# Attention and gated MLP on one core: where the gain's multiplications stand in block 2, and how the last tokens of batch 0 are laid out

## The chip, the cores and the metric

The kernel runs on one core of one Trainium2 chip. A core has a matrix engine (TensorE, "PE" in the profile; its weight loads are "PEld"), three engines for elementwise work (VectorE "DVE", ScalarE "ACT", GpSimd "POOL"), a queue engine (SyncE, "SP") and 16 DMA engines that move data between device memory and the on-chip memory of 128 partitions. The products of TensorE go to PSUM, a memory of eight banks.

The metric is the device time of one execution in microseconds. The kernel before takes 338.99 us, the median of 3 runs (338.89 to 339.11).

## What is computed

```python
# q, k, v: (8 batches, 8 heads, 576 tokens, 64)   fp32;  g_norm: (64,)
kv  = einsum('bhsd,bhse->bhde', k, v)             # linear attention, no softmax
out = einsum('bhsd,bhde->bhse', q, kv)
rms = sqrt(mean(out * out, axis=-1, keepdims=True) + 1e-06)
x   = (out / rms * g_norm)                        # -> (4608 tokens, 512)
g   = x @ w_gate;  val = x @ w_val                # 512 -> 1536
ffn = (gelu(g) * val) @ w_out                     # 1536 -> 512
y   = x + sigmoid(x @ w_res) * ffn
```

The kernel works in nine blocks: block b (0 to 7) takes the first 512 tokens of batch b, and block 8 takes the last 64 tokens of all batches. `kv` needs all 576 tokens of a batch, so each batch's last 64 tokens of k and v are loaded apart. While TensorE does the MLP of one block, the other engines and some slots of TensorE do the attention of the next.

## The kernel before

The opening (batch 0). Loads are issued on the SyncE queue in this order; `th_all` is a buffer that the MLP uses later, borrowed here for the fp32 last tokens.

```python
first_raw, first_last = [], []
for which in "kv":
    t = hid_of[which]
    first_last.append(t[:, 2 * H * NJ * D :][:, 0 : 2 * H * D].rearrange("p (j h d) -> p j h d", j=2, h=H))
    first_raw.append([th_all[:, 2 * len(first_raw) + i, :] for i in range(2)])

def load_first_last(half):                      # four heads of k, and of v
    hs = slice(half * HH, (half + 1) * HH)
    for i, t in enumerate((k, v)):
        nc.sync.dma_start(                      # 32 partitions x 4 heads x (2 tokens x 64)
            out=first_raw[i][half][0 : R // 2, :].rearrange("p (h x) -> p h x", h=HH),
            in_=t[0, hs, M0:S, :].rearrange("h (p j) d -> p h (j d)", j=2),
        )

for which, t in (("q", q), ("k", k), ("v", v)):
    load_first(which, t, 0, HH)                 # heads 0 to 3, 512 KB each
    if which == "k":
        load_first_last(0)
for pr in range(NP // 2, NP):                   # head pairs 2 and 3, 256 KB each
    load_first("q", q, 2 * pr, 2 * pr + 2)
    load_first("k", k, 2 * pr, 2 * pr + 2)
    if pr == NP // 2:
        load_first_last(1)
    load_first("v", v, 2 * pr, 2 * pr + 2)
# [cut: fp32 loads of the first columns of w_gate and w_val, on the same queue]
```

The rows of `first_last` that no token fills are zeroed; a cast brings the tokens to fp16; `f_kv` sums the product over the tokens of a head pair, and `f_kv_out` keeps the two diagonal 64x64 blocks of the 128x128 result with a mask:

```python
for t in first_last:
    nc.vector.memset(t, 0.0)
# [cut]
def f_cast_last(i, half, copy):
    hs = slice(half * HH, (half + 1) * HH)
    copy(out=first_last[i].rearrange("p j h d -> p h j d")[0 : R // 2, hs, :, :],
         in_=first_raw[i][half][0 : R // 2, :].rearrange("p (h j d) -> p h j d", h=HH, j=2))

def f_kv(pr):
    # [cut: four matmuls over the first 512 tokens]
    for j in range(2):
        kl, vl = (t[:, j].rearrange("p h d -> p (h d)")[:, cs] for t in first_last)
        nc.tensor.matmul(ps, lhsT=kl, rhs=vl, start=False, stop=(j == 1))

def f_kv_out(pr):
    nc.vector.tensor_tensor(out=s0["kv2"][:, pr, :], in0=first["kv", pr], in1=mask, op=ALU.mult)
```

The order of the opening is a list of words: a name, a number (head pair, half or count) and the engine (A ScalarE, D VectorE, P GpSimd). qc, kc, vc are casts; lk, lv the casts of the last tokens; qT, qo the transpose of q and its copy; kv, kvo the product and its masked copy; o the product with q; sq, rd, rt, ri, t the normalisation; xT, xo the transpose of x; g, v the first MLP products; wg, wv, wcg, wcv loads and casts of weights; warm matmuls on zeros that keep TensorE busy.

```python
opening = """
qc1P qc0A qT1 qT0 kc1P kc0A qo0D warm3 lv0D lk0P qo1A warm3 vc1D vc0A kv1 qc2A kv0 kvo1 kvo0 o1 kc2P qT2
lk1P lv1D sq1 qo2D o0 warm3 warm2 vc2P sq0 rd1 kv2 qc3P rt1 kvo2 rd0 kc3A qT3 wg1 wv1 ri1 o2 rt0 t1 warm3 warm1 sq2 vc3D
rd2 qo3A xT1 kv3 wg2 wcg0P rt2 kvo3 ri0 ri2 warm2 o3 t2 xo1A wcg1P sq3a wcv0P sq3b g1 xT2 rd3a wcv1P rd3b
wv2 t0 xo2A wg3 wv3 v1 xT0 rt3 ri3 xo0A g2 v2 t3a t3b xT3a xT3b g0 xo3aA xo3bD gelu v0 g3a v3a g3b v3b
"""
```

A block of the MLP has 12 slots, one for each group of 128 columns. In each, TensorE makes two products (`gps`, `vps`, eight matmuls), ScalarE the gelu, VectorE the product of the two; four PSUM banks take turns. Further work is put in after a slot's own:

```python
def m_act(blk, f, gps, vps):
    nc.scalar.activation(out=ge, in_=gps, func=AF.Gelu)                        # L345
    nc.vector.tensor_tensor(out=hids[blk][:, f, :], in0=ge, in1=vps, op=ALU.mult)  # L346

def a_norm(b, j0, j1):                       # slot 7 of block 2, for batch 3
    nc.vector.tensor_scalar(out=m, in0=ss, ...)                # L275
    nc.vector.tensor_scalar(out=yy.bitcast(I32), in0=m.bitcast(I32), ...)      # L276
    # [cut: L279, then nine small instructions L281 to L283]

def a_x(b, j):                               # one row of x, times g, in place   # L317
    nc.vector.tensor_tensor(out=t_t[blk][:, jj, :], in0=t_t[blk][:, jj, :], in1=g16, op=ALU.mult)
```

Block 1's x for TensorE takes g in a transpose copy, so its rows in `t_t[1]` are without g and are multiplied only for the residual addition. Block 1's output is finished during block 2, on GpSimd (`fin`, L492), and stored:

```python
if later:                                     # block 1 alone
    at(blk + 1, 5, lambda: fin((0, 0)))       # res_all += t_t[1], rows 0 and 1
    at(blk + 1, 6, lambda: fin((0, 1)), lambda: store(0))
    at(blk + 1, 9, lambda: fin((1, 0)))       # rows 2 and 3
    at(blk + 1, 10, lambda: fin((1, 1)), lambda: store(1))
# [cut]
if blk == 2:
    for j, g in enumerate(rows):              # rows: a_x(1, 0) to a_x(1, 3)
        plan.setdefault(3 + j, []).append(g)
```

In block 2 the other additions to slots are: the kv product of batch 3 and its copy (slot 1), GpSimd's issue of batch 4's loads (slot 2), the products with q and their squares and sums (slots 2 to 5), `a_norm` (7), a sum of halves of `hid` (8, L425), and the scaling and the multiplication by g of batch 3's rows (9 and 10).

Of the kernel before, what the change touches and what calls it, by code (L numbers as in the profile page):

```python
# [8 lines left out]
FP32 = mybir.dt.float32  # L9
# [3 lines left out]
ALU = mybir.AluOpType  # L13
# [5 lines left out]
def kernel(  # L19
# [15 lines left out]
    nc = tc.nc  # L35
    P = nc.NUM_PARTITIONS
    B, H, S, D = q.shape
# [4 lines left out]
    NJ = 4  # L42
    M0 = NJ * P
    R = S - M0
    RP = R // NJ
    HH = H // 2
    WCS = (256, 256, 512, 512)

    consts = ctx.enter_context(tc.tile_pool(name="consts", bufs=1))
# [92 lines left out]
    th_all = finp.tile([P, NJ, C], FP32, bufs=1, name="th")  # L142
# [634 lines left out]
    for which in "kv":  # L777
        if which == "k":
            t = hidp.tile([P, NF, NJ * P], FP16, tag="hid", name=which + "f").rearrange("p a b -> p (a b)")
        else:  # L780
            t = hid_s
# [7 lines left out]
    first_raw, first_last = [], []  # L789
    for which in "kv":  # L790
        t = hid_of[which]
        first_last.append(t[:, 2 * H * NJ * D :][:, 0 : 2 * H * D].rearrange("p (j h d) -> p j h d", j=2, h=H))
        first_raw.append([th_all[:, 2 * len(first_raw) + i, :] for i in range(2)])

    def load_first_last(half):
        hs = slice(half * HH, (half + 1) * HH)
        for i, t in enumerate((k, v)):
            nc.sync.dma_start(
                out=first_raw[i][half][0 : R // 2, :].rearrange("p (h x) -> p h x", h=HH),
                in_=t[0, hs, M0:S, :].rearrange("h (p j) d -> p h (j d)", j=2),  # L800
            )

# [20 lines left out]

    zeros = consts.tile([P, C], FP16, name="zeros")
    nc.vector.memset(zeros, 0.0)
    for t in first_last:
        nc.vector.memset(t, 0.0)
    mask = consts.tile([P, P], FP32, name="mask")
    nc.vector.memset(mask, 0.0)
    nc.vector.memset(mask[0:D, 0:D], 1.0)  # L830
# [6 lines left out]
    nc.vector.memset(one32, 1.0)  # L837
    ident = consts.tile([P, P], FP16, name="ident")
    nc.vector.tensor_copy(out=ident, in_=ident32)
    grow32 = consts.tile([1, 2, D], FP32, name="grow32")  # L840
    nc.vector.tensor_copy(out=grow32, in_=grow[:, None, :].to_broadcast([1, 2, D]))
    grow16 = consts.tile([1, H, D], FP16, name="grow16")
# [34 lines left out]
                in_=src.rearrange("p h (j d) -> p h j d", j=NJ)[:, hs, :, :],  # L877
            )

    def f_cast_last(i, half, copy):  # L880
        hs = slice(half * HH, (half + 1) * HH)
        copy(
            out=first_last[i].rearrange("p j h d -> p h j d")[0 : R // 2, hs, :, :],
            in_=first_raw[i][half][0 : R // 2, :].rearrange("p (h j d) -> p h j d", h=HH, j=2),
        )

    def f_qT(pr):
        q16 = b16_t[0, "q"].rearrange("p j h d -> p j (h d)")
# [7 lines left out]
    def f_kv(pr):  # L896

        first["kv", pr] = ps = pattn.tile([P, P], FP32, tag="at", name="kvp")
        k16 = b16_t[0, "k"].rearrange("p j h d -> p j (h d)")
        hs, cs = of_pair(pr)  # L900
        for j in range(NJ):
            nc.tensor.matmul(
                ps, lhsT=k16[:, j, cs], rhs=b16_t[0, "v"][:, hs, j * D : (j + 1) * D], start=(j == 0), stop=False
            )
        for j in range(2):
            kl, vl = (t[:, j].rearrange("p h d -> p (h d)")[:, cs] for t in first_last)
            nc.tensor.matmul(ps, lhsT=kl, rhs=vl, start=False, stop=(j == 1))

    def f_kv_out(pr):
# [65 lines left out]
    def f_piece(word):  # L975

        name = word.rstrip("0123abADP")
        rest = word[len(name) :]
        pr = int(rest[0])
        j0, j1 = {"a": (0, NJ // 2), "b": (NJ // 2, NJ)}.get(rest[1:2], (0, NJ))  # L980
        eng = rest[-1:]
        if name in ("qc", "kc", "vc"):
            f_cast(name[0], pr, engines[eng])
        elif name in ("lk", "lv"):
            f_cast_last("kv".index(name[1]), pr, engines[eng])
        elif name == "warm":
            keep_warm(pr)
        elif name == "wg":
            load_wg(pr)
        elif name == "wv":  # L990
            load_wv(pr)
        elif name in ("wcg", "wcv"):
            cs = slice(2 * pr, 2 * pr + 2)
            engines[eng](out=(wg_c if name == "wcg" else wv_c)[0][:, cs, :], in_=w_raw[name[-1]][:, cs, :])
        elif name == "qo":
            f_qT_out(pr, engines[eng])
        elif name in ("qT", "kv", "kvo", "o", "rt", "ri"):
            {"qT": f_qT, "kv": f_kv, "kvo": f_kv_out, "o": f_o, "rt": f_sqrt, "ri": f_rinv}[name](pr)
        elif name in ("sq", "rd", "t", "xT"):
            {"sq": f_sq, "rd": f_red, "t": f_t, "xT": f_xT}[name](pr, j0, j1)  # L1000
        elif name == "xo":
            f_xT_out(pr, j0, j1, eng)
        elif name == "g":
            f_mm(wg_c, 0, pr, j0, j1)
        elif name == "v":
            f_mm(wv_c, 1, pr, j0, j1)
# [15 lines left out]


    opening = """
    qc1P qc0A qT1 qT0 kc1P kc0A qo0D warm3 lv0D lk0P qo1A warm3 vc1D vc0A kv1 qc2A kv0 kvo1 kvo0 o1 kc2P qT2
    lk1P lv1D sq1 qo2D o0 warm3 warm2 vc2P sq0 rd1 kv2 qc3P rt1 kvo2 rd0 kc3A qT3 wg1 wv1 ri1 o2 rt0 t1 warm3 warm1 sq2 vc3D
    rd2 qo3A xT1 kv3 wg2 wcg0P rt2 kvo3 ri0 ri2 warm2 o3 t2 xo1A wcg1P sq3a wcv0P sq3b g1 xT2 rd3a wcv1P rd3b
    wv2 t0 xo2A wg3 wv3 v1 xT0 rt3 ri3 xo0A g2 v2 t3a t3b xT3a xT3b g0 xo3aA xo3bD gelu v0 g3a v3a g3b v3b
    """
# [122 lines left out]
    for blk in range(B + 1):  # L1152
        plan = plans[blk]
        if blk == 0:
            slots = [first_gval, None]
            slots += [lambda: m_gval(0, 2, pattn, "at")]
            slots += [lambda f=f: m_gval(0, f) for f in range(3, NF)]
            outs, stores = out_by_f(0)
            slots += outs
            for b in range(2, B):  # L1160
                plan_attn(b)
            plan[5] = [lambda j=j: a_x(0, j) for j in range(NJ)]
        else:
            slots = [lambda f=f: m_gval(blk, f) for f in range(NF)]
            sevens = blk in LAST
            if sevens:
                slots = [None] * NF
                ends = banks_of(blk)
                mid = [lambda: s_begin(blk)]
                for g in range(NF // GF):  # L1170
                    slots[GF * g] = lambda g=g: gv_group(blk, g, ends[g], mid if g == 2 else ())
            if blk == 1:
                slots[0] = lambda: m_gval(1, 0, pattn, "at")
                plan.setdefault(3, []).append(lambda: (wo_sums(1), wo_sums(3)))
            outs = []
            slots += [lambda i=i: outs[i]() for i in range(4 if blk < B else 2)]
            if not sevens:
                plan.setdefault(NFH + 2, []).insert(0, lambda: s_begin(blk))
            for j, f in enumerate(sums_in.get(blk, ())):
                plan.setdefault(SUM_SLOTS[j], []).append(f)  # L1180
            if blk + 1 in LAST:
                for ahead_of, f in zip(("00", "01", "22", "11"), token_sums(blk + 1, nc.vector)):
                    amid_out.setdefault(blk, {}).setdefault(ahead_of, []).append(f)

            def products(blk=blk, outs=outs):
                s_rest(blk)
                if blk not in LAST:
                    out_at[blk] = banks_behind()
                if blk + 1 == LAST[0]:
                    out_at[blk].update({j: pattn.turn[j] for j in range(NJ)})  # L1190
                if blk < B:
                    outs.extend(out_by_products(blk, blk == 1, out_at[blk], amid_out.get(blk, {})))
                else:
                    outs.extend(out_last(blk, out_at[blk]))

            plan.setdefault(NF - 1, []).append(products)
            for j, fs in enumerate(late):
                plan.setdefault(j, []).extend(fs)
            late = []
            if blk == 2:  # L1200
                for j, g in enumerate(rows):
                    plan.setdefault(3 + j, []).append(g)
        if blk == 0:
            new_block(1)
            more, rows = attn_plan_1()
            for i, fs in more.items():
                plan.setdefault(i, []).extend(fs)
        elif blk + 1 < B:
            new_block(blk + 1)
        for s in range(len(slots)):  # L1210
            if slots[s] is not None:
                slots[s]()
            for f in plan.pop(s, []):
                f()
            if blk == 0 and s == 2:
                nc.gpsimd.dma_start(out=wr16, in_=moe_w_res.rearrange("(cc p) c -> p cc c", p=P))
                load_batch(1)
                for f0, f1 in ((0, 2), (2, 4), (4, 8), (8, NF)):
                    load_wo(f0, f1)
        assert not plan  # L1220
        if blk == 0:
            late = [[g] for g in stores] + [[] for _ in range(NJ)]
# [30 lines left out]
```

## Time and profile before

| | us |
|---|---|
| time, median of 3 | 338.99 |
| span of the profiled execution | 337.3 |
| TensorE busy | 326.6 |
| VectorE, ScalarE, GpSimd busy | 255.4, 161.5, 109.3 |
| opening: first MLP product of slot 2 begins | 22.76 |
| block 2: from its first product to its first output product | 92.86 to 120.24 |

Times are counted from the start of the span. L with a number is a line of the kernel. A row of a timeline has start, duration, engine, line, operation, what it writes and reads, shapes, a count, and in brackets the idle time ahead of it with what ended it. A row of waits has who waited and for whom, the total in us, how often, and the longest. A row of stretches has the stretch, its length, the busy time of TensorE, its weight loads, VectorE, ScalarE and GpSimd with counts, the granted clock, the mean busy share of the 16 DMA engines and the rate in GB/s. Busy time of an engine that others wait for is not by itself what sets the end.

### The profile page before, as it was taken

How to read it: one execution, taken by the hardware profiler on the slowest of the kernel's cores; microseconds unless marked ns; L12 is line 12 of the kernel's file. 1: busy time of each engine (PE TensorE's matmuls, PEld its weight loads, DVE VectorE, ACT ScalarE, POOL GpSimd, SP SyncE). 2: the span in 40 equal slices, each digit the busy share in tenths (PEclk: the TensorE clock that was granted, in tenths of full speed). 3: DMA queues.
4: the chain of work that ended last, by engine and by line, in shares of the span. 5: the costliest groups of instructions: out<-in, count | busy, mean ns of one | idle time of the engine just before them, and what ended most of it. 6: DMA issues, size and time to landing. Idle time of an engine off the chain costs nothing.

```text
span 337.3 us, 6523 instructions
## 1 busy us (share of the span) xinstructions
PE 326.6 (97%) x2576; PEld 200.9 (60%) x2576; DVE 255.4 (76%) x498; ACT 161.5 (48%) x289; POOL 109.3 (32%) x127
## 2 busy tenths in 40 slices
PE   8889999999999999999999999999999999999993
PEld 3444454444844476447644674458444888788872
DVE  6755449669859988788677968796789877777754
ACT  3663384264335361536163535343454376646760
POOL 2783161990053108400650057003200251142232
PEclk9999999999999999999999999999999999999998
DMA  8999999669489272983498339924300330011004
GB/s 239 319 197 204 195 203 158 171 101 151 83 134 171 105 115 104 174 85 77 135 176 94 63 102 179 136 45 98 126 0 5 74 125 2 2 54 73 0 2 124
DMA packets 76688, 38.82 MB, mean 115 GB/s; under 512 B 42098, under 2 KB 74354, under 8 KB 76658
## 3 DMA queue, kind: packets, MB, share of 16 engines
q0 software_dynamic: 38752, 17.17, 40.4%
q1 hardware_dynamic: 37328, 20.71, 22.4%
q10 hardware_dynamic: 578, 0.52, 0.5%
q8 instruction: 20, 0.33, 0.4%
q14 instruction: 10, 0.08, 0.1%
HBM read 38.80 MB, written 9.44 MB: 143 GB/s over the span
## 4 chain that ended last, share of the span: by engine, by line
PE 90%; DVE 4%; DMA 3%; issue 0%; ACT 0%; POOL 0%; SPq 0%; DVEq 0%
PE gps L357 21%; PE vps L357 20%; PE wA L452 11%; PE rps L377 8%; PE fps L394 3%; PE Av L692 3%; PE Ag L692 3%; PE wE L452 3%; PE wD L452 3%; PE wF L452 3%; PE w L452 2%; DMA hid_s<-in_v_dram 2%; PE kvp L208 2%; PE Fv L692 2%; PE Fg L692 2%; DMA kf<-in_k_dram 2%
## 5 line engine op out<-in xcount | busy, mean ns | idle before, releaser
L345 ACT ACTIVATE ge<-gps 128x512 f16<-128x512 f32 x84 | 50.2, 598 | 98.4 <-PE gps L357 96.7
L357 PE MATMUL vps<-xT,wv 128*128 128x512 f16 x328 | 84.2, 379 | 0.8 <-DVE hid L346 0.8
L357 PE MATMUL gps<-xT,wg 128*128 128x512 f16 x328 | 84.3, 380 | 0.0
L346 DVE TENSOR_TENSOR hid<-ge,vps 128x512 f16<-128x512 f16 x84 | 57.4, 684 | 32.6 <-PE vps L357 28.7
L492 POOL TENSOR_TENSOR osb<-osb,t 128x512 f32<-128x512 f32 x28 | 35.3, 1277 | 138.0 <-DVE osb L488 132.4
L357 PEld LDWEIGHTS <-wv 128*128 128x128 f16 x328 | 32.1, 98 | 39.7 <-issue 1.1
L357 PEld LDWEIGHTS <-wg 128*128 128x128 f16 x328 | 30.7, 98 | 34.5 <-issue 0.2
L452 PEld LDWEIGHTS <-hid_s 128*128 128x128 f16 x384 | 37.6, 98 | 4.5 <-issue 0.2
L377 PE MATMUL rps<-wr,xT 128*128 128x512 f16 x144 | 32.5, 379 | 0.0
L452 PEld LDWEIGHTS <-hid 128*128 128x128 f16 x288 | 28.2, 98 | 5.5 <-issue 0.8
L386 ACT ACTIVATE th<-rps 128x512 f32<-128x512 f32 x36 | 21.5, 599 | 16.4 <-PE rps L377 16.4
L377 PEld LDWEIGHTS <-xT 128*128 128x128 f16 x144 | 14.1, 98 | 16.6
L245 DVE TENSOR_REDUCE ss<-sq 128x8 f32<-128x512 f32 x32 | 20.6, 680 | 2.9 <-ACT sq L243 2.8
L452 PE MATMUL wA<-wo_ts,hid_s 128*128 128x256 f16 x168 | 20.6, 273 | 0.0
L692 PEld LDWEIGHTS <-ws 128*128 128x128 f16 x192 | 18.8, 98 | 2.2
L391 ACT ACTIVATE th<-th 128x512 f32<-128x512 f32 x36 | 19.9, 623 | 0.0
L303 DVE TENSOR_TENSOR t<-op,ny 128x512 f16<-128x512 f32 x28 | 17.9, 685 | 0.1
L243 ACT ACTIVATE sq<-op 128x512 f32<-128x512 f32 x28 | 15.3, 598 | 4.5 <-PE op L226 4.1
L317 DVE TENSOR_TENSOR t<-t,g 128x512 f16<-128x512 f16 x36 | 15.4, 478 | 0.1
L425 DVE TENSOR_TENSOR hid_s<-hid 128x1536 f16<-128x1536 f16 x16 | 15.3, 954 | 0.2
L729 POOL TENSOR_TENSOR hid<-ge,c 128x512 f16<-128x512 f16 x6 | 7.0, 1163 | 23.4 <-ACT ge L723 23.4
L394 PE MATMUL fps<-wo,hid 128*128 128x512 f16 x48 | 11.2, 379 | 0.0
(172 smaller groups left out, 472.5 us busy)
## 6 DMA issues: line engine op xcount, KB each, us to landing
out_dram<-osb SPq DMA_DIRECT2D x14, 512.0 KB, 2.6
qraw<-in_q_dram POOLq DMA_DIRECT2D x7, 512.0 KB, 8.1
k<-in_k_dram POOLq DMA_DIRECT2D x7, 512.0 KB, 9.7
v<-in_v_dram POOLq DMA_DIRECT2D x7, 512.0 KB, 11.5
wg<-in_moe_w_gate_dram POOLq DMA_DIRECT2D x2, 512.0 KB, 8.2
wv<-in_moe_w_val_dram POOLq DMA_DIRECT2D x2, 512.0 KB, 9.0
wo<-in_moe_w_out_dram POOLq DMA_DIRECT2D x2, 512.0 KB, 13.6
out_dram<-osb SPq DMA_DIRECT2D x4, 256.0 KB, 2.9
```

The costliest lines, as they stand in the source:

```text
L245: nc.vector.tensor_reduce(out=out_, in_=sq, op=ALU.add, axis=mybir.AxisListType.X)
L303: nc.vector.tensor_tensor(out=t, in0=o, in1=scale, op=ALU.mult)
L345: nc.scalar.activation(out=ge, in_=gps, func=AF.Gelu)
L346: nc.vector.tensor_tensor(out=hids[blk][:, f, :], in0=ge, in1=vps, op=ALU.mult)
L357: nc.tensor.matmul(ps[:, j0 * P : j1 * P], lhsT=w[:, cc, :], rhs=xT_t[blk][:, j0:j1, cc, :], start=(cc == 0 and j0 == 0), stop=(cc == NP - ...
L377: nc.tensor.matmul(rps, lhsT=xT_t[blk][:, j, cc, :], rhs=wr16[:, cc, :], start=(cc == 0), stop=(cc == NP - 1),)
L386: nc.scalar.activation(out=th, in_=rps, func=AF.Tanh, scale=0.5)
L391: nc.scalar.activation(out=th, in_=th, func=AF.Copy, scale=0.5, bias=0.5)
L394: nc.tensor.matmul(fps, lhsT=hids[blk][:, f, j * P : (j + 1) * P], rhs=wo16[:, f, :], start=(f == 0), stop=(f == NF - 1))
L452: nc.tensor.matmul(ps[:, e - es[0], :], lhsT=a[:, f, e * P : (e + 1) * P], rhs=b[:, f, :], start=(start and e == es[0] and f == 0), stop=( ...
L492: nc.gpsimd.tensor_tensor(out=res_all[of], in0=res_all[of], in1=t_t[blk][of], op=ALU.add)
L692: nc.tensor.matmul(out_[:, r, :], lhsT=lhsT, rhs=rhs, start=(first and r == 0 and c == 0), stop=(c == 1), skip_group_check=True,)
```

## The change

It has two parts. In block 2 the four multiplications of block 1's rows by g stand in slots 0 to 3 instead of 3 to 6, ahead of the sums of squares. In the opening, the last 64 tokens of batch 0's k and v are loaded onto 128 partitions instead of 32, one row of two tokens of one head to each partition[...]. Rows of four heads then lie mixed over the partitions, so k is multiplied, for each head, by a column `of_head` that is 1 on that head's partitions and 0 on the others; v is copied twice, for both heads of a pair, and the mask on the result removes what doesn't belong. The two buffers no longer need to be zeroed. The cast of the second half of v moves to ScalarE and to a later place.

```diff
+        rest = t[:, 2 * H * NJ * D :]
+        if which == "k":
+            first_last.append(rest[:, 0 : 2 * H * D].rearrange("p (j h d) -> p j h d", j=2, h=H))
+        else:
+            first_last.append(rest[:, 0 : 8 * D].rearrange("p (i j e d) -> p i j e d", i=2, j=2, e=2))
+        first_raw.append([th_all[:, 2 * len(first_raw) + i, 0 : 2 * D] for i in range(2)])
 ...
-                out=first_raw[i][half][0 : R // 2, :].rearrange("p (h x) -> p h x", h=HH),
+                out=first_raw[i][half],
                 in_=t[0, hs, M0:S, :].rearrange("h (p j) d -> p h (j d)", j=2),
 ...
-    for t in first_last:
-        nc.vector.memset(t, 0.0)
 ...
+    of_head = consts.tile([P, HH], FP32, name="of_head")
+    nc.vector.tensor_reduce(
+        out=of_head, in_=ident32.rearrange("p (r h) -> p h r", h=HH), op=ALU.add, axis=mybir.AxisListType.X
+    )
 ...
-    def f_cast_last(i, half, copy):  [cut]
+    def f_k_last(half, engs):
+        raw_ = first_raw[0][half].rearrange("p (j d) -> p j d", j=2)
+        for j, eng in enumerate(engs):
+            eng.tensor_tensor(
+                out=first_last[0][:, j, half * HH : (half + 1) * HH, :],
+                in0=raw_[:, j, None, :].to_broadcast([P, HH, D]),
+                in1=of_head[:, :, None].to_broadcast([P, HH, D]),
+                op=ALU.mult,
+            )
+
+    def f_v_last(half, copy):
+        raw_ = first_raw[1][half].rearrange("p (j d) -> p j d", j=2)
+        copy(out=first_last[1][:, half], in_=raw_[:, :, None, :].to_broadcast([P, 2, 2, D]))
 ...
-            kl, vl = (t[:, j].rearrange("p h d -> p (h d)")[:, cs] for t in first_last)
+            kl = first_last[0][:, j].rearrange("p h d -> p (h d)")[:, cs]
+            vl = first_last[1][:, pr // 2, j].rearrange("p e d -> p (e d)")
 ...
+        elif name == "lk":
+            f_k_last(pr, (nc.gpsimd if eng == "P" else nc.vector, nc.vector))
+        elif name == "lv":
+            f_v_last(pr, engines[eng])
 ...
-    qc1P qc0A qT1 qT0 kc1P kc0A qo0D warm3 lv0D lk0P qo1A warm3 vc1D vc0A kv1 qc2A kv0 kvo1 kvo0 o1 kc2P qT2
-    lk1P lv1D sq1 qo2D o0 warm3 warm2 vc2P sq0 rd1 kv2 qc3P rt1 [cut]
+    qc1P qc0A qT1 qT0 kc1P kc0A qo0D warm3 lk0D lv0P qo1A warm3 vc1D vc0A kv1 qc2A kv0 kvo1 kvo0 o1 kc2P qT2
+    lk1P sq1 qo2D o0 warm3 warm2 vc2P sq0 lv1A rd1 kv2 qc3P rt1 [cut]
 ...
                 for j, g in enumerate(rows):
-                    plan.setdefault(3 + j, []).append(g)
+                    plan.setdefault(j, []).append(g)
```

## The prediction

> **What bounds the kernel now.** First the page: its busy lines, then the waits of TensorE, longest first.
>
> ```profile
> PE 326.6 (97%) x2576; PEld 200.9 (60%) x2576; DVE 255.4 (76%) x498; ACT 161.5 (48%) x289; POOL 109.3 (32%) x127
> ```
>
> ```profile
> PE gps L967 <- DVE t L941: 1.3, 1, 1.3
> ...
> PE vps L357 <- DVE hid L346: 0.8, 1, 0.8
> PE kvp L902 <- POOL v L873: 0.7, 1, 0.7
> PE kvp L902 <- DVE v L873: 0.4, 1, 0.4
> ...
> PE wA L452 <- DVE hid L346: 0.2, 1, 0.2
> ```
>
> TensorE is idle for 337.3 - 326.6 = 10.7 us. The table of stretches places it: 1.2 us at the start, 21.50 - 18.41 = 3.1 us in the rest of the opening (1.2 to 22.7 us), 1.0 us in block 2 (93 to 121 us), 5.4 us after the last product, and 210.00 of 210 us busy between 121 and 331. So only the opening and block 2 can give anything, and a gain there should reach the end undiminished. In the opening TensorE also runs matmuls on zeros to fill time, so idle time understates what can be saved: what counts is the chain of arrivals. The chain that ended last begins so (start, us, what):
>
> ```profile
> 1.27 5.13 DMA kf<-in_k_dram
> 6.42 5.28 DMA hid_s<-in_v_dram
> ```
>
> The third load of v lands at 11.70, GpSimd casts it at 11.75, TensorE starts `kv2` at 12.42. The stretches of a quarter microsecond show why loads are late (last two columns: DMA share, GB/s):
>
> ```profile
> 5.00:5.25 0.25, 0.25 (x3) 0.01 (x1) 0.25 (x1) 0.17 (x1) 0.19 (x1) 1.00 1.09 352
> ...
> 6.25:6.50 0.25, 0.25 (x5) 0.25 (x3) 0.00 (x0) 0.08 (x1) 0.05 (x1) 1.00 1.12 209
> ...
> 10.00:10.25 0.25, 0.25 (x8) 0.25 (x7) 0.13 (x1) 0.00 (x0) 0.00 (x0) 1.00 1.17 205
> ...
> 11.50:11.75 0.25, 0.25 (x2) 0.00 (x0) 0.25 (x2) 0.00 (x0) 0.03 (x1) 1.00 1.10 389
> ```
>
> The full rate is 385 GB/s, but from 5.5 to 7.0 and from 9.25 to 10.9 it is about 205. These two dips start with the two pairs of last-token loads (`th`, 64 KB each, onto 32 partitions). In the packet records, 1 KB packets take 46 ns outside the dips and 84 to 96 inside; the 512-byte packets of `th` take 27 ns when they begin. Their count there (77 in a quarter of a microsecond at 27 to 29 ns) is what eight engines can do, not sixteen, while 1 KB packets go on at a half rate: I read it as eight engines carrying `th`, the others running ahead and then losing step.
>
> In block 2 I read VectorE and GpSimd side by side (start, us, engine and line):
>
> ```profile
> 107.92 0.78 DVE L317 TENSOR_TENSOR t<-t,g 128x512 f16<-128x512 f16 x1
> 108.84 0.69 DVE L346 TENSOR_TENSOR hid<-ge,vps 128x512 f16<-128x512 f16 x1
> 109.45 0.53 DVE L275 TENSOR_SCALAR nm<-ss 128x40 f32<-128x40 f32 x1
> 110.01 1.08 DVE L276 TENSOR_SCALAR ny<-nm 128x40 int32<-128x40 int32 x1
> ...
> 105.97 2.45 POOL L492 TENSOR_TENSOR osb<-osb,t 128x512 f32<-128x512 f32 x2 [5.25 <-DVE t L317]
> 108.78 2.27 POOL L492 TENSOR_TENSOR osb<-osb,t 128x512 f32<-128x512 f32 x2 [0.36 <-DVE t L317]
> ```
>
> In other blocks L275 takes 0.18 us and L276 0.18; here 0.53 and 1.08, and the second ends at 111.09, when GpSimd's addition ends (111.05). The normalisation thus loses 0.35 + 0.90 = 1.25 us to GpSimd. Slot 8's `hid`, next in VectorE's order, comes at 113.11 though its product was ready by 110.5; TensorE's `vps` of slot 10 needs the bank it frees and starts at 113.84, after 0.79 us idle. The same delay carried to slot 11's `hid` (119.50 to 120.19) costs 0.19 us before `wA`.
>
> **What the Trainium skill says.** "SBUF — State Buffer", section "Who interferes with whom": VectorE's `tensor_scalar` can use a two-port mode, which takes exclusively the port pair shared with GpSimd; whoever starts first keeps it for its whole instruction. The trace agrees: the 0.53 and the 1.08 both end with a GpSimd addition. It also says that a VectorE operation with two SBUF inputs contends with GpSimd's reads; L317 at 107.92 (0.78 instead of 0.42) fits. Section "Door 1: The DMA port swizzle": partitions 0 to 31 reach 8 of 16 ports, with 189 GB/s measured against 328 for 128; the dips' 205 against 385 is that ratio. "DMA: Bandwidth & Descriptors", section "The descriptor swizzle": partitions 0 to 31 are written by engines 0 to 7, which fits the eight counted above; why 1 KB packets stay slow after `th` is done, neither page nor trace tells.
>
> **The change, part by part: opening.** (a) Removed: two memsets of 0.48 us on VectorE at 1.19 and 1.73; added: one reduction of 128x128 to 128x4. I estimate it at 0.25 us (a 128x256 reduction has a mean of 0.41 here, a 128x128 cast takes 0.21). The copies of g then come some 0.75 us earlier; their 256 bytes moved at 1.70, long before the copy at 3.03. TensorE's chain of g and three zero matmuls (3.43 to 5.86) ends near 5.1, and the transposes of q start at 5.3, held by the cast of q that ends at 5.19, not at 5.65: 0.35 us earlier.
>
> (b) Each pair of last-token loads becomes 256 packets of 512 bytes over all engines: 256 x 27 ns / 16 = 0.43 us without a dip. Between 4.75 and 7.25 there were 528 packets of 1 KB and these 256; at full rate (94 per 0.25 us) 1.40 + 0.43 = 1.83 us instead of 2.5: 0.67 less. Between 8.5 and 11.0, 512 and 256: 1.36 + 0.43 = 1.79, so 0.71 less. First v then lands at 8.47 - 0.6 = 7.9, the second k at 9.3 instead of 10.32, the third v at 10.35 instead of 11.70, weights some 1.35 earlier.
>
> (c) New products. First half: two VectorE multiplications of 128x256 (about 0.33 us each, half a 128x512 `t` of 0.69) replace its one cast of 0.51; GpSimd's copy replaces its cast of 0.60. They read SBUF together and may hold each other for 0.3 to 0.6 us, so the v cast that starts at 8.49 now starts about 8.2, and `kv1` at 8.65 instead of 8.97. Second half: one multiplication on GpSimd (half of 1.16 to 1.28, say 0.6, as the cast before), one on VectorE, and v's copy goes to ScalarE, free after 11.0. What leaves is VectorE's wait of 1.17 us for `th` ahead of the cast at 11.30, with `qT` and a reduction behind it.
>
> (d) `kv2`: GpSimd casts k at 9.35 to 9.95, multiplies to 10.6, casts v to 11.2 instead of 12.36. TensorE's work up to `kv2` ended at 11.76; earlier by the shift of `kv1` this is 11.45. So `kv2` comes near 11.45 instead of 12.42. VectorE's product of it, at 12.95, starts the nearly gapless row of VectorE work up to 18.18; it comes near 11.95. GpSimd's issue of weight loads (12.95) moves by about 1.1, wgf lands near 13.6, so no later load holds. The opening gives **0.95 us**.
>
> **Block 2.** The four multiplications L317 leave slots 3 to 6 for 0 to 3. VectorE has gaps of 1.04, 1.82 and 1.03 us ahead of the `hid` of slots 1 to 3, so three cost nothing. GpSimd, waiting 5.25 us for the first two rows, is free at 100.72: its four additions (2.45 + 2.27 = 4.7 us) then run from 100.8 to about 106. The fourth row, at 103.4, may be held up to 0.9 us behind one of them; VectorE catches up, since slots 4 to 6 lose three rows of 0.34 us, and slot 7's `hid` waits for its `vps` at 108.84 as before. The normalisation then has GpSimd idle and takes 1.25 us less: slot 8's `hid` at 111.86, done at 112.5, ahead of TensorE's need at 113.05. The 0.79 goes. Slot 11's `hid` ends at 118.94, the gate products at 119.26: the 0.19 goes too. **0.98 us.** Sum: 338.99 - 0.95 - 0.98 = 337.06, rounded to 337.1.
>
> **Rivals.** (1) The dips stay, because 512-byte packets spread over 16 engines still meet on ports or in HBM. For it: 1 KB packets stay at 88 ns for 0.75 us after `th`'s last packet at 6.1. Against: no other stretch before 15 us dips. The opening then gives 0.3, the time is 337.7. (2) A new wait replaces v's: two-input operations of VectorE and GpSimd block one another in both halves, or ScalarE's new copy delays the square root. For it: blocked cases of 0.4 and 0.9 us above. It would take 0.3 to 0.6 off: 337.5. (3) GpSimd's earlier additions only move the collision to VectorE's slots 3 to 5, or the two earlier stores (512 KB) delay batch 4's loads. Those land by 109.46 and are used after 119, so the stores are hidden; the additions would have to cost over 2 us. The block gives nothing then: 338.0. (4) The opening gains more, since loads come 1.35 us earlier and VectorE is freer: 336.5.
>
> **Range and chances.** I hold block 2 for the surer part (0.98 at 85%), the opening for 0.95 with a spread of 0.3 to 1.4. This gives 337.1, 336.4 to 338.2. Faster by over 2% means below 332.2, nearly 7 us, more than all idle time outside start and end; slower by over 2% means a stall of 7 us, which nothing points to.
>
> **What would show it.** Opening: no dip near 6 and 10 us; the third v landing near 10.4; `kv2` near 11.45; the first L357 product near 21.8 instead of 22.76. Block 2: L275 and L276 at 0.18 each, additions done before 107, no wait of `vps` for `hid`. I am wrong if the rate still falls to 205 GB/s, if `kv2` waits for `kf` or `hid_s` pieces, or if additions still overlap the normalisation.

## The result, and the profile after

The changed kernel takes 337.31 us (median of 4 runs, 337.21 to 337.85); the kernel before took 339.05 in the same comparison (4 runs, 338.89 to 339.24). The ratio is 0.9952, with a 95% interval of 0.9934 to 0.9969. That is 1.7 us less, within 2%. The prediction was 337.1, with 336.4 to 338.2 as its range.

TensorE's waits in the changed kernel (us in total, times, longest):

```profile
PE gps L982 <- DVE t L956: 1.3, 1, 1.3
...
PE kvp L916 <- DVE v L879: 0.3, 1, 0.3
...
PE kvp L916 <- POOL v L879: 0.2, 1, 0.2
```

Both waits of block 2 (`vps` for `hid` 0.8, `wA` for `hid` 0.2) are gone. Of the opening's waits for v, 0.7 and 0.4 became 0.2 and 0.3. The wait of 1.3 for `t`, which the change doesn't touch, stands as it was.

Block 2 in the timeline of the changed kernel, VectorE and then GpSimd (start, us, engine, line, in brackets the idle time ahead):

```profile
103.22 0.59 DVE L317 TENSOR_TENSOR t<-t,g 128x512 f16<-128x512 f16 x1
...
108.71 0.69 DVE L346 TENSOR_TENSOR hid<-ge,vps 128x512 f16<-128x512 f16 x1 [1.04 <-PE vps L357]
109.32 0.18 DVE L275 TENSOR_SCALAR nm<-ss 128x40 f32<-128x40 f32 x1
109.53 0.18 DVE L276 TENSOR_SCALAR ny<-nm 128x40 int32<-128x40 int32 x1
...
111.73 0.68 DVE L346 TENSOR_TENSOR hid<-ge,vps 128x512 f16<-128x512 f16 x1
...
101.17 2.33 POOL L492 TENSOR_TENSOR osb<-osb,t 128x512 f32<-128x512 f32 x2
103.88 2.27 POOL L492 TENSOR_TENSOR osb<-osb,t 128x512 f32<-128x512 f32 x2 [0.37 <-DVE t L317]
```

The additions end at 106.15, three microseconds ahead of the normalisation. L275 and L276 take 0.18 each instead of 0.53 and 1.08, and slot 8's `hid` comes 3.02 us after slot 7's instead of 4.27.

The opening, in stretches of a quarter microsecond (last two columns: DMA share, GB/s):

```profile
6.25:6.50 0.25, 0.25 (x5) 0.25 (x4) 0.00 (x0) 0.00 (x0) 0.00 (x0) 1.00 1.06 334
...
10.00:10.25 0.25, 0.20 (x5) 0.12 (x3) 0.21 (x2) 0.12 (x1) 0.00 (x0) 1.00 1.12 352
...
11.50:11.75 0.25, 0.25 (x3) 0.13 (x2) 0.25 (x2) 0.25 (x2) 0.25 (x2) 1.00 1.12 352
```

The dips to 205 GB/s are gone. But the rate behind them, which was 389 at 11.5 us before, is now 352. And in this profile the opening is hardly shorter: the first MLP product of slot 2 starts at 22.61 instead of 22.76. The first q landed at 5.10 us, not at 4.52 as in the profile before, and the profiled run was the slowest of the four (337.85). Over all profiles of this study the first q lands anywhere from 4.5 to 5.2 us, though it is the first load in all of them, and what follows moves with it. So openings are compared here at like landings of the first q.

### The profile page after: what moved, and what is told of

It is laid out like the page before. It is cut to its first block, busy times and chain, and to the rows that moved or that the text cites. A ratio compares the mean times of both kernels' runs of the same rounds, so it can differ in the third digit from the quotient of the medians.

```text
span 335.9 us, 6522 instructions
## 1 busy us (share of the span) xinstructions
PE 326.7 (97%) x2576; PEld 200.8 (60%) x2576; DVE 254.1 (76%) x498; ACT 161.5 (48%) x290; POOL 109.7 (33%) x127
## 4 chain that ended last, share of the span: by engine, by line
PE 93%; DVE 2%; DMA 2%; SPq 1%; POOL 0%; issue 0%; ACT 0%; DVEq 0%
PE gps L357 22%; PE vps L357 21%; PE wA L452 11%; PE rps L377 9%; PE fps L394 3%; PE Av L692 3%; PE Ag L692 3%; PE wE L452 3%; PE wF L452 3%; PE wD L452 3%; PE w L452 2%; DMA kf<-in_k_dram 2%; PE kvp L208 2%; PE Fv L692 2%; PE Fg L692 2%; PE op L226 1%
## 6 DMA issues: line engine op xcount, KB each, us to landing
v<-in_v_dram POOLq DMA_DIRECT2D x7, 512.0 KB, 11.5
```

## Experiments

The sum of two parts hides which of them was sized rightly. The theory is the prediction's: GpSimd's additions blocked the normalisation in block 2, and slow loads held `kv2` in the opening. The rivals were that the rows' own time on VectorE mattered in slots 3 to 6, and that in the opening it was not the loads but VectorE's wait for `th`, or TensorE's own fill work.

### The two parts apart

Rows alone (the opening as before):

```diff
-                    plan.setdefault(3 + j, []).append(g)
+                    plan.setdefault(j, []).append(g)
```

> The kernel before with block 1's rows times g in slots 0 to 3 of block 2, and nothing of the opening changed. If the collision of GpSimd's additions with the normalisation was the cost (theory), TensorE's waits of 0.79 and 0.19 us go, the first output product of block 2 comes 1.0 to 1.3 us earlier, and the time is 337.8 (337.6 to 338.1). If most of the gain of the change came from the opening (rival), it is 338.6 or more.

The opening alone: the changed kernel with that one line as it was.

> The kernel before with the opening of the change alone (128 partitions, mask of rows, v's copy on ScalarE), rows in slots 3 to 6 as before. If the two parts add up, the opening is worth what e1 leaves of the whole: 0.5 us, 338.5 (338.2 to 338.7). The prediction's 0.95 would make it 338.0. The rate after the first pair of last-token loads: 350 GB/s if the new layout leaves the DMA engines out of step for good, 385 if the 350 of the changed kernel's profile was of that one run.

The changed kernel once more:

> The changed kernel as it is, once more, for a second profile and a time beside e1 and e2. 337.3 (337.1 to 337.6). If the late landing of the first q (5.10 us instead of 4.52) in its first profile was chance, the first MLP product of slot 2 comes near 22.1 instead of 22.61; if it belongs to the change, near 22.6 again.

| kernel | ratio to before | 95% interval | us of 339.19 |
|---|---|---|---|
| rows alone | 0.9960 | 0.9945 to 0.9975 | -1.36 |
| opening alone | 0.9984 | 0.9977 to 0.9990 | -0.54 |
| both | 0.9949 | 0.9934 to 0.9963 | -1.73 |

The parts add up (-1.90 against -1.73, well inside the intervals). By the medians alone the three differences are 1.22, 0.55 and 1.41. Either way, the shift of one index brings some 70%. The 337.78 of the changed kernel lies above the 337.6 that was put as its upper end.

Its first q landed at 5.17 and slot 2 started at 22.84, not near 22.1, which by its expectation would mean that the late landing belongs to the change. But the kernel with the opening alone has the same loads in the same order: there q landed at 4.58, and slot 2 started at 22.14, 0.62 ahead of before. Nor is the new layout needed for a late q: it landed at 5.05 in a kernel below that has no last tokens at all. What makes it late stays open.

The rate did stay at the lower level. The kernel with the opening alone, ahead of the first last-token loads and behind both pairs, and the second stretch in the kernel before:

```profile
3.00:4.75 1.75, 1.75 (x6) 0.65 (x5) 1.36 (x6) 0.15 (x1) 0.12 (x1) 1.00 1.09 380
...
11.00:13.50 2.50, 2.16 (x20) 1.28 (x19) 1.78 (x6) 1.64 (x6) 2.50 (x5) 1.00 1.10 349
```

```profile
11.00:13.50 2.50, 1.69 (x18) 1.00 (x17) 1.98 (x5) 1.10 (x3) 2.24 (x4) 1.00 1.09 383
```

Before, the rate recovers to 383; with the new layout it goes from 380 to 349 and stays there. In the packet records of the opening alone a 1 KB packet takes 46 ns ahead of the last-token loads and 51 behind them.

### Is it the additions, or the rows?

The kernel before, with GpSimd's four additions for block 1 left out (the output of block 1 lacks its residual x), rows still in slots 3 to 6:

```diff
-            at(blk + 1, 5, lambda: fin((0, 0)))
-            at(blk + 1, 6, lambda: fin((0, 1)), lambda: store(0))
-            at(blk + 1, 9, lambda: fin((1, 0)))
-            at(blk + 1, 10, lambda: fin((1, 1)), lambda: store(1))
+            at(blk + 1, 6, lambda: store(0))
+            at(blk + 1, 10, lambda: store(1))
```

> The kernel before without GpSimd's four additions for block 1 (its output lacks the residual x), rows in slots 3 to 6 as before. If the additions' overlap with the normalisation is what costs (theory), the two instructions L275 and L276 take 0.18 us each, TensorE's two waits in block 2 go, and the time is as in e1, 337.8 (337.6 to 338.1), though VectorE does the rows where it did. If the rows' own time on VectorE in slots 3 to 6 was the cost (rival), TensorE still waits 0.8 us and the time stays at 339.0.

The ratio is 0.9958 (0.9947 to 0.9969), -1.42 us, the same as with early rows. From its timeline, VectorE:

```profile
108.02 0.42 DVE L317 TENSOR_TENSOR t<-t,g 128x512 f16<-128x512 f16 x1
108.95 0.69 DVE L346 TENSOR_TENSOR hid<-ge,vps 128x512 f16<-128x512 f16 x1 [0.50 <-PE vps L357]
109.55 0.18 DVE L275 TENSOR_SCALAR nm<-ss 128x40 f32<-128x40 f32 x1
109.77 0.18 DVE L276 TENSOR_SCALAR ny<-nm 128x40 int32<-128x40 int32 x1
```

VectorE does every row where it did, and there are 0.50 us to spare ahead of slot 7's `hid`. TensorE has no wait left in the block. So the rows' own time cost nothing.

Then the reverse: rows early, but the additions held back until VectorE has written the last sum of squares.

```diff
-            at(blk + 1, 5, lambda: fin((0, 0)))
+            at(blk + 1, 5, lambda: nc.gpsimd.tensor_copy(out=hold, in_=st[blk + 2]["ss"][0:1, NJ, 0:1]), lambda: fin((0, 0)))
```

(and the rows in slots 0 to 3, as in the kernel with rows alone)

> The kernel before with rows in slots 0 to 3 (as e1), but GpSimd first reads one number of batch 3's last sum of squares, which VectorE writes just ahead of the normalisation, so that its four additions start near 107 and run to 112. Theory (collision): early rows are then worth nothing, L275 and L276 are stretched by 1 us or more together, TensorE waits again, and the time is that of before or up to 1 us more, 339.0 to 340.0. Rival (the rows' place on VectorE): the gain of e1 stays, 337.9.

The ratio is 1.0024 (1.0002 to 1.0047), 340.04 us at the median. Its timeline, VectorE, GpSimd and TensorE:

```profile
109.54 2.10 DVE L275 TENSOR_SCALAR nm<-ss 128x40 f32<-128x40 f32 x1
...
107.11 4.48 POOL L492 TENSOR_TENSOR osb<-osb,t 128x512 f32<-128x512 f32 x4
...
114.61 1.02 PE L357 MATMUL vps<-xT,wv 128*128 128x512 f16 x4 [1.47 <-DVE hid L346]
```

L275, an instruction on 40 numbers a partition, lasts until the fourth addition ends (109.54 + 2.10 = 111.64, against 107.11 + 4.48 = 111.59). With the rows early, the gain of the rows is lost and a bit more. Both directions say the same: what counts in block 2 is whether GpSimd's additions lie across the normalisation. The rows' early place matters because the additions wait for the rows.

### The opening: loads, or VectorE's wait?

The kernel before with one word moved, v's second last tokens cast on ScalarE later; loads on 32 partitions:

```diff
-    lk1P lv1D sq1 qo2D o0 warm3 warm2 vc2P sq0 rd1 kv2 [cut]
+    lk1P sq1 qo2D o0 warm3 warm2 vc2P sq0 lv1A rd1 kv2 [cut]
```

> The kernel before with one word moved: the cast of v's second last tokens on ScalarE after sq0 instead of on VectorE after lk1; loads on 32 partitions as before. Theory (the late v is the chain): VectorE's wait of 1.17 us goes, but kv2 still waits for the third v at 11.7, so the time falls by 0.1 at most, 339.0. Rival (VectorE's wait was what cost): it falls by 0.4 or more, as e2 did.

The ratio is 0.9993 (0.9978 to 1.0007): nothing. VectorE's wait is gone from its place and turns up at the masked copy of `kv2`:

```profile
10.91 0.69 DVE L927 TENSOR_REDUCE ss<-sq 128x8 f32<-128x512 f32 x1
12.89 0.29 DVE L910 TENSOR_TENSOR kv<-kvp,mask 128x128 f16<-128x128 f32 x1 [1.29 <-PE kvp L907]
```

The new layout in the old order of words (lv on VectorE, k's half on GpSimd first, v's second half on VectorE again), with the rows back in slots 3 to 6; the edit is against the changed kernel:

```diff
-    [cut] qo0D warm3 lk0D lv0P qo1A [cut]
-    lk1P sq1 qo2D o0 warm3 warm2 vc2P sq0 lv1A rd1 kv2 [cut]
+    [cut] qo0D warm3 lv0D lk0P qo1A [cut]
+    lk1P lv1D sq1 qo2D o0 warm3 warm2 vc2P sq0 rd1 kv2 [cut]
 ...
-                    plan.setdefault(j, []).append(g)
+                    plan.setdefault(3 + j, []).append(g)
```

> The kernel before with the new layout of the last tokens (128 partitions, mask of rows, no memsets), but the words in the old order: lv on VectorE ahead, lk on GpSimd and VectorE, v's second half on VectorE after lk1. Theory (the loads are what counts): v's third load lands 0.8 us earlier, at equal landing of the first q, and the time is within 0.2 of e2, 0.4 to 0.6 below before. Rival: without the move to ScalarE the layout is worth less than 0.2.

The third v lands at 11.03 (first q at 4.57), 0.7 earlier, and the ratio is 0.9977 (0.9964 to 0.9991), -0.8 us with an interval that holds the 0.54 of the opening as it is. So the opening's gain is the layout's; moving v's copy to ScalarE adds nothing that these runs can measure.

### How much could the loads give?

The kernel before without the last tokens of batch 0: no loads, memsets, casts and matmuls of them (batch 0's kv lacks 64 of 576 tokens).

```diff
-        if which == "k":
-            load_first_last(0)
 ...
-        if pr == NP // 2:
-            load_first_last(1)
 ...
-    [cut] lv0D lk0P qo1A [cut]
-    lk1P lv1D sq1 [cut]
+    [cut] qo1A [cut]
+    sq1 [cut]
```

> The kernel before without the last tokens of batch 0's k and v: no loads, casts, memsets and matmuls of them (the output of batch 0 lacks 64 tokens of 576 in kv). It bounds what any layout of these loads can give. No dips at all: 385 GB/s throughout, the third v lands near 9.9, kv2 comes when TensorE's own fill work ends, near 11.3 to 11.5, and the time is 1.0 us below before (0.8 to 1.3). If it is no more than 0.6 below, the loads were not what limits and the new layout already gives all of it.

The ratio is 0.9980 (0.9964 to 0.9995), -0.7 us, with runs from 337.8 to 339.84; the interval takes in both what was expected and the limit of 0.6, and also the 0.54 of the new layout. The profile says more. It is one with a late first q (5.05). The third v landed so early (9.77) that its cast ended at 10.43, and yet:

```profile
6.59 2.77 PE L846 MATMUL idle<-zeros 128*128 128x512 f16 x6
...
10.68 1.24 PE L846 MATMUL idle<-zeros 128*128 128x512 f16 x5
...
11.76 0.39 PE L896 MATMUL kvp<-v,k 128*128 128x128 f16 x4
...
13.82 1.16 DVE L867 CAST v<-hid_s 128x512 f16<-128x512 f32 x1
```

`kv2`, put near 11.3 to 11.5, waits for TensorE's own five fill matmuls and starts at 11.76. Later the last cast of v takes 1.16 us instead of 0.42 on VectorE while GpSimd casts the first weights (13.49 to 14.68). Slot 2 starts at 22.71, no earlier than in the changed kernel at a like landing of q (22.61 at 5.10). So with these loads gone, TensorE's fill and VectorE's next collision take the gain.

Part of it belongs to this profile and not to the kernel. TensorE's fill matmuls start 0.43 us apart at first and 0.22 apart later, and the quicker pace comes at another time in each profile: near 7.9 us in the kernel before, 8.5 with the opening alone, 9.3 here. The six fill matmuls ahead of `kv1`, 2.77 us here, took less before:

```profile
6.50 2.12 PE L852 MATMUL idle<-zeros 128*128 128x512 f16 x6
```

So these runs don't show how much a kernel without the loads could gain; the next one, with all loads in place and q 0.3 earlier, starts slot 2 earlier by 0.7.

### Three attempts to go further

k's second last tokens on VectorE alone, three of eleven fill matmuls left out:

```diff
-    [cut] lk0D lv0P qo1A warm3 vc1D [cut]
-    lk1P sq1 qo2D o0 warm3 warm2 vc2P sq0 lv1A rd1 kv2 [cut]
+    [cut] lk0D lv0P qo1A warm2 vc1D [cut]
+    lk1D sq1 qo2D o0 warm3 vc2P sq0 lv1A rd1 kv2 [cut]
```

> The changed kernel with k's second last tokens on VectorE alone (GpSimd free for v's cast) and three of the eleven fill matmuls between the first transposes and kv2 left out. If TensorE's own fill work and GpSimd's 0.78 us ahead of v's cast are the next limits of the opening, kv2 comes 0.2 to 0.4 us earlier and the time is 337.1 to 337.4 where the changed kernel has 337.3 to 337.8. If the landing of v is the limit, nothing moves.

337.12 us, ratio 0.9927 (0.9910 to 0.9943); `kv2` starts at 11.63, slot 2 at 21.97. At a first q of 4.73 this is 0.17 ahead of the opening alone, at 4.58. In addition to that, the third q loaded after the third v:

```diff
+        if pr > NP // 2:
+            load_first("q", q, 2 * pr, 2 * pr + 2)
 ...
+        if pr == NP // 2:
+            load_first("q", q, 2 * pr, 2 * pr + 2)
 ...
-    [cut] kv1 qc2A kv0 kvo1 kvo0 o1 kc2P qT2
-    lk1D sq1 qo2D o0 warm3 vc2P sq0 lv1A rd1 kv2 qc3P rt1 kvo2 rd0 [cut]
+    [cut] kv1 kv0 kvo1 kvo0 o1 kc2P
+    lk1D sq1 o0 warm3 vc2P sq0 lv1A rd1 kv2 qc2A kvo2 qT2 qo2D qc3P rt1 rd0 [cut]
```

> As e9, and the third q is loaded after the third v, with its cast, transpose and copy after kv2. v then lands 0.7 us earlier (256 KB at 350 GB/s). If the landing of v is the limit, kv2 comes 0.5 to 0.7 us earlier than in e9 and the time falls by as much, to 336.8; VectorE's gap of 0.68 us ahead of the masked copy bounds it. If q's later way to the copy delays o2, the time is that of e9 or worse.

337.83 us, ratio 0.9957 (0.9944 to 0.9969). `kv2` did start 0.6 us earlier, at 11.03, but slot 2 later, at 22.39. VectorE's timeline:

```profile
12.36 0.42 DVE L911 COPY qT<-qtp 128x512 f16<-128x512 f16 x1 [0.35 <-PE qtp L908]
12.70 0.68 DVE L945 TENSOR_REDUCE ss<-sq 128x8 f32<-128x512 f32 x1
```

The sum of squares now stands behind q's copy and starts at 12.70, where it started at 12.37 without this step. And the third v cast on VectorE, on top of the first attempt:

```diff
-    [cut] warm3 vc2P sq0 [cut]
+    [cut] warm3 vc2D sq0 [cut]
```

> As e9, and the third v is cast on VectorE (0.42 us) instead of GpSimd (0.62). If GpSimd's cast is what kv2 now waits for (0.56 us in e9), kv2 comes 0.2 us earlier, but VectorE's sum of squares behind it comes 0.3 later; the time is within 0.2 of e9's, 337.0 to 337.3, and 0.7% below before again. If VectorE is the next limit, it is 0.2 to 0.4 slower than e9.

337.19 us, ratio 0.9940 (0.9920 to 0.9961). The time is no different from the first attempt, as expected. But `kv2` came no earlier, at 11.71: VectorE was taken by k's multiplications and q's copy, and started v's cast at 11.15, though v had landed at 10.81. Both attempts are faster than the kernel before; their medians (337.12, 337.19) are below those of the changed kernel (337.31 and 337.78), but the intervals overlap (0.9910 to 0.9943 against 0.9934 to 0.9969), so a gain on the changed kernel is likely and not shown.

### Why the rate stays low

The changed kernel with the last-token loads issued from ScalarE's queue:

```diff
-            nc.sync.dma_start(
+            nc.scalar.dma_start(
                 out=first_raw[i][half],
```

> The changed kernel with the four last-token loads issued from ScalarE's queue instead of SyncE's: the same packets, in rings of their own, sent early. If the lasting 350 GB/s comes from short packets in the same ring as the long ones, the rate after 6.5 us is 385; if it comes from the layout on the engines, 350 as before. The time may go either way by 0.5 us (all four loads now stand ahead of v): 337.0 to 338.2.

337.72 us, ratio 0.9943 (0.9923 to 0.9963). The stretch behind the loads:

```profile
11.00:13.50 2.50, 2.23 (x21) 1.26 (x20) 1.47 (x4) 1.54 (x5) 2.50 (x5) 1.00 1.10 349
```

349 again. So it doesn't come from short packets in the same queue as the long ones. What in the new layout keeps the rate down stays open. So does why the old layout made dips: that eight of the 16 DMA engines carried those loads was read from a packet count and from a likeness of two ratios, and the packet records don't name the engine. The runs show only that the dips go with the loads onto 32 partitions.

## Why the prediction was right, and where not

**Block 2** went by the steps as written, down to the rows: additions done before 107 (106.15), L275 and L276 at 0.18, the fourth row held behind an addition but without effect (0.59 instead of 0.42; 0.9 had been allowed). Only the size was off, and on the low side: rows alone brought 1.36 where 0.98 was put. The interval of that (0.85 to 1.87) takes in 0.98, but the profiles are closer. The mis-sized term is the cost of the two waits, which was taken from the idle time recorded. The distances between starts give it better. TensorE before, and then with rows alone:

```profile
112.03 1.03 PE L357 MATMUL gps<-xT,wg 128*128 128x512 f16 x4
113.84 1.02 PE L357 MATMUL vps<-xT,wv 128*128 128x512 f16 x4 [0.79 <-DVE hid L346]
...
120.24 1.47 PE L452 MATMUL wA<-wo,hid 128*128 128x256 f16 x12 [0.19 <-DVE hid L346]
```

```profile
119.05 1.47 PE L452 MATMUL wA<-wo,hid 128*128 128x256 f16 x12
```

In slot 10, `gps` started at 112.03 and `vps` at 113.84, 1.81 apart; undisturbed they are 0.86 apart, so the wait cost 0.95, not 0.79. From the first product with `w_res` to `wA` it was 3.81 before and 3.52 in the kernel with early rows, so 0.29, not 0.19. That makes 1.24, and the span between block 2's first product and `wA` in the two profiles differs by as much: 120.24 - 92.86 = 27.38 against 119.05 - 92.92 = 26.13.

**The opening** was put at 0.95 and measured 0.54 (0.34 to 0.78), 0.62 in the profile with a like landing of q. Three terms of the sum fell short; read in the kernel with the opening alone:

- Step (a), transposes of q 0.35 us earlier: they started at 5.65, as before. The copies of g were done 0.8 us earlier (2.79 instead of 3.57), but TensorE took up the product with g at 3.43 in both kernels, since its first five fill matmuls last from 1.19 until then. The wait named in the profile (`gcp` for `grow`) was no cause.
- Step (b), no dip and full rate: the dips went, the full rate didn't come back. The second k landed at 9.79 instead of 10.32, not at 9.3, and the third v at 10.96 instead of 11.70, not at 10.35. The lower rate explains about 0.35 us of the 0.6 missing (an estimate: 1280 KB at 349 instead of 385 GB/s); the rest isn't traced. The first fp32 weights, put some 1.35 earlier, landed at 14.73 instead of 14.96.
- Step (d), `kv2` at 11.45: it started at 11.81. GpSimd began with k 0.5 later than put, since k landed later, and its cast of v had to wait for its multiplication, which took 0.78 us and not 0.6:

```profile
9.84 0.61 POOL L881 CAST k<-kf 128x512 f16<-128x512 f32 x1 [2.72 <-DMA kf<-in_k_dram]
10.42 0.78 POOL L890 TENSOR_TENSOR kf<-th,of_head 128x256 f16<-128x256 f32 x1
11.15 0.60 POOL L879 CAST v<-hid_s 128x512 f16<-128x512 f32 x1
11.81 0.38 PE L916 MATMUL kvp<-v,k 128*128 128x128 f16 x4 [0.22 <-POOL v L879]
```

The first three instructions, with the landing of k ahead of them, are the chain that ends last in this part. TensorE would have been ready as put: its last fill matmul started at 11.21, and the next product follows 0.22 later where nothing holds it (11.54 and 11.76 in the kernel without last tokens), so 11.43. GpSimd's chain cost the other 0.4.

**The rivals.** The first (the dips stay) came half true in another form: no dips, but a tenth of the rate lost for good. The second (two-input operations block one another) came true for GpSimd's multiplication, by 0.2 rather than 0.3 to 0.6: it took 0.78 beside one of VectorE (10.06 to 10.73) and 0.61 in the run with loads from ScalarE's queue, where VectorE's was done before it began. No wait on ScalarE's copy shows. The third did not happen. The fourth (the opening gains more) fell with the rate. That the total fell so close to 337.1 is in part luck: block 2 was 0.3 to 0.4 under, the opening 0.3 to 0.4 over.

## What to carry to other kernels

When a short instruction takes several times its usual time (0.53, 1.08 and 2.10 us here instead of 0.18), look at what GpSimd was doing at that moment, and then at what GpSimd had been waiting for: moving that earlier can pull two engines apart at no cost. Take the price of a TensorE wait from the distance between starts, against an undisturbed pair, not from the idle time in the record. And where an engine fills its time with idle work in its own order, count that work as part of the path before crediting it with an earlier arrival.

## What was not expected

- After the 512 packets of 512 bytes onto 128 partitions, 1 KB packets took 51 ns instead of 46, at 349 GB/s instead of 383, up to the next kind of load at 15 us. It showed in all profiles with the new layout and in none without it, from either queue.
- The first load of q landed between 4.5 and 5.2 us after the start of the span, though it is the first load in every kernel here, and the opening moved with it.
- With the additions held back, a VectorE instruction of 0.18 us (L275) stood for 2.10 us behind additions on GpSimd that follow one another without a gap: it wasn't let in between the third and the fourth. In the kernel before it was: there L275 ended at 109.98, just as the first of two such additions gave way to the second (109.94). What decides this stays open.
